# A recurrence with 64-step chunks, then a routed expert layer: other order of loads, zeroed pads, weights and last units

## The chip, the cores and the metric

The kernel runs on one core of a Trainium2 chip. The metric is the device time of one execution in microseconds (us), lower is better. The kernel before takes 865.59 us, the median of three runs (860.16 to 867.03).

The engines are TensorE (PE, with its weight loads shown apart as PEld), VectorE (DVE), ScalarE (ACT), GpSimd (POOL) and SyncE (SP), which here only issues DMAs. Each engine works through its own list of instructions in order. An instruction whose input is not ready holds up all that stands behind it on the same engine.

## The reference, cut to what matters

```python
for t in range(S):                                    # B=4, H=8, S=768, D=40
    y[:, :, t] = np.einsum('bhd,bhde->bhe', rt, state)
    Sa = np.einsum('bhde,bhe->bhd', state, at)
    state = state * wt[:, :, None, :] - np.einsum('bhd,bhe->bhde', Sa, bt) + np.einsum('bhd,bhe->bhde', vt, kt)
x = y.transpose(0, 2, 1, 3).reshape(3072, 320)
logits = x @ w_gate                                   # 8 experts
e = argmax(logits); g = softmax(logits)[e]
out = g * (relu(x @ w1[e]) @ w2[e])                   # w1: 8 x 320 x 1024, w2: 8 x 1024 x 320
```

A recurrence runs over 768 steps for 32 heads. Its output is the input of a layer in which each of 3072 rows goes to one of eight experts.

## The kernel before, in words

The work has three stages. The first is the recurrence, cut into chunks of 64 steps. A unit is one chunk of two batches with all their heads; there are 24 units (`NU`, line 316), and units 2c and 2c+1 are chunk c of the two pairs of batches. `unit(u)` (line 416) writes down the steps of one unit:

- seven loads, each of four DMAs of 40 KB (`load`, line 432): the decays `dec`, the vectors B and K into the one tile `KB`, A, V twice (`V2`, `Vu`) and R. For the first two units B, A and R are issued by ACT, all others by SP.
- preparation: a backward scan of the decays (`rv`, line 453), two small operations (line 457), a forward scan (`q`, line 461), both scans on DVE; two multiplications of halves of `KB` by `rv` (line 468) and one of A by `q` (line 470), on POOL.
- on TensorE the products of K and A and of B and A (lines 492 and 506), then a chain of squarings that inverts a triangular matrix (lines 518 to 584), the terms that need the state of the chunk before (lines 614 to 656), `p_z` (line 668), the output and new state `p_y` (line 692), and `p_x` (line 722), which turns the output into rows and multiplies it by the gate's weights. DVE and ACT copy or mask what comes out. SP stores the rows (line 758).

The heads of a tile are eight segments. In `dec`, A, `q`, `rv` and `pc` segment 2p+q holds pair p of batch q, so the segments of the two batches alternate. `dec` has segments of 65 columns, one for a reset and 64 decays. A DMA of `dec` fills the segments of one batch and one half of the partitions, so the two DMAs of a half interleave (`by_q`, line 440).

Tiles have pads (partitions 40 to 63 and 104 to 127) that must be zero, and in `dec` one. The tiles lie in rings of two or three buffers (lines 337 to 363), and lines 365 to 387 clear the pads of each buffer once. `fill_turn_gate` (line 158) prepares the gate's weights with two DMAs issued by POOL, `turn_sign` (line 166) negates them, and `route_constants` (line 137) makes the constants of the routing on POOL.

The order of this stage is made by a planner at build time, `in_order` (line 224). Each `Step` has a rank, an engine (or `ANY` for ACT or DVE), a guessed cost, and what it reads and writes (`Held`). The planner goes through time and takes the step that can start first; among those that can start at the same moment it takes the one of the lowest rank. The rank is the unit's number for the work of the unit, u-3 for its loads, u-1 for its preparation, u+1 for what follows `p_x`. For TensorE steps a term `uneven` is added to the rank: it compares a step's cost with its number of instructions `n` times `PACE`, so that steps with many short instructions alternate with steps of few long ones. What the planner guesses decides only the order. On the chip each instruction waits for its real inputs, which the framework finds from the regions that instructions write and read.

The weights of expert 0 are loaded by `fetch` (line 176) in four DMAs after half of the units (lines 767 to 772).

The second stage is the routing (lines 780 to 886), the third the experts (lines 889 to 987). There the weights of expert e+2 are loaded while e and e+1 run.

Of the kernel before, what the change touches and what calls it, by code (L numbers as in the profile page):

```python
# [23 lines left out]
def kernel(  # L24
# [151 lines left out]
    def fetch(pool, w1, w2):  # L176
# [4 lines left out]
        nc.sync.dma_start(t1[:], w1[: Dm - 64].rearrange("(a p) f -> p a f", p=128))  # L181
        for i in range(2):
            nc.sync.dma_start(
                t3[i * 64 : (i + 1) * 64], w1[Dm - 64 :].rearrange("p (k i f) -> i p k f", i=2, f=128)[i],
            )
        nc.sync.dma_start(t2[:], w2.rearrange("(a p) d -> p a d", p=128))
# [8 lines left out]
    PACE = 0.0134  # L195
# [28 lines left out]
    def in_order():  # L224
# [31 lines left out]
        while ready:  # L256
            times = sorted({f for f in bank_free if f is not None})
            best = None
            for s, r in ready.items():
                new = [h for h in s.ps if h.at is None]  # L260
                for e in ((ACT, DVE) if s.eng == ANY else (s.eng,)):
# [14 lines left out]
                    uneven = 2 * abs(even + s.cost - s.n * PACE) if s.n else 0.0  # L276
# [41 lines left out]
    with tc.tile_pool(name="ring", bufs=1) as ring, \  # L318
# [21 lines left out]
        r_KB = Ring("KB", [NP, 2, 2, C], 3, 2)  # L340
# [29 lines left out]
        for i, (t, held) in enumerate(r_dec.bufs):  # L370
# [45 lines left out]
        def unit(u):  # L416
# [9 lines left out]
            def head(t, p, q, par):  # L426
                return t[halves[par], 2 * p + q, :]
# [21 lines left out]
            load(other, 1 + A, by_q(Aq), hA)  # L449
# [14 lines left out]
            for i in range(2):  # L464
# [576 lines left out]
```

## Time and profile before

| What | Value |
|---|---|
| Runs of the kernel | 865.59 us median (860.16 to 867.03) |
| The profiled execution's own time | 866.43 us |
| Its span in the profile | 864.7 us |
| Granted TensorE clock, mean over the span | 0.946 |

The profile shows one execution. Times in it count from the start of its span; 1.7 us of the execution's own time lie outside the span. A granted clock of 1.00 is 2.4 GHz, 0.50 is 1.2 GHz; numbers between are means over a stretch in which both occurred. Busy time counts the time in which at least one instruction of the engine ran. A count of matmuls beside it (x) says how much was done. In a list of waits, "DVE rv L453 <- DMA dec" is idle time of DVE before an instruction of line 453, ended by the landing of a DMA into `dec`. A name such as SPq or ACTq is the sequencer of that engine, which issues DMAs.

### The profile page before, as it was taken

The page shows a single profiled execution, that of the slowest core. Times are in us where ns is not written, and L with a number is a line of the kernel's source. Part 1 is how long each engine was busy: PE and PEld are TensorE (multiplying, and loading weights), DVE is VectorE, ACT ScalarE, POOL GpSimd, SP SyncE. Part 2 cuts the span into 40 slices and gives each one's busy share as a digit, 9 for nine tenths or more (in the row PEclk, how much of TensorE's full clock was granted, in tenths as well). Part 3 has the DMA queues.
Part 4 walks back from the last instruction along what each step waited for, and adds up shares of the span by engine and source line. Part 5 has one row for each costly group of instructions (what it writes and reads, how often), then busy time and mean ns, then how long its engine had stood idle before and what let it go on. Part 6 is the DMA issues. An engine that isn't in the chain of part 4 may idle for free.

```text
span 864.7 us, 38029 instructions
## 1 busy us (share of the span) xinstructions
PE 767.2 (89%) x17128; PEld 607.9 (70%) x17128; DVE 464.2 (54%) x991; ACT 229.7 (27%) x495; POOL 178.5 (21%) x226
## 2 busy tenths in 40 slices
PE   0779899999999997999999997159999999999995
PEld 0668788989888997898889886147655655655643
DVE  8575688878888788687787773621120120120110
ACT  0233443434343442344333431001011111111010
POOL 9712101112012221121121100160401401101001
PEclk9998999999999999899999996566999999999999
DMA  3333323323232336323322100740424424202000
GB/s 86 81 68 68 69 51 70 84 51 88 59 76 62 78 76 172 72 63 73 82 62 64 29 13 11 226 146 10 148 68 136 140 68 147 77 6 87 16 7 24
DMA packets 136293, 65.16 MB, mean 75 GB/s; under 512 B 116585, under 2 KB 131967, under 8 KB 136128
## 3 DMA queue, kind: packets, MB, share of 16 engines
q1 hardware_dynamic: 128848, 52.26, 23.8%
q0 software_dynamic: 3200, 9.45, 3.5%
q8 instruction: 135, 2.21, 1.1%
q10 hardware_dynamic: 4080, 0.98, 0.5%
q14 instruction: 30, 0.25, 0.1%
HBM read 54.01 MB, written 9.31 MB: 73 GB/s over the span
## 4 chain that ended last, share of the span: by engine, by line
issue 36%; PE 32%; DVE 11%; POOL 8%; DMA 8%; SPq 3%; ACT 1%; POOLq 0%; DVEq 0%; ACTq 0%
PE ps L406 27%; DMA dec<-in_packed_dram 6%; POOL out_dram L936 3%; SPq L437 3%; PE ps L603 3%; POOL xg L894 3%; DVE X L516 2%; PE ps L593 2%; DVE X L513 1%; DVE q L461 1%; DVE rv L453 1%; DVE TT L516 1%; DVE M L573 1%; DVE ZU L676 1%; ACT X L401 1%
## 5 line engine op out<-in xcount | busy, mean ns | idle before, releaser
L406 PE MATMUL ps<-X 64*64 64x64 f32 (+1 forms) x6144 | 153.5, 243 | 10.2 <-issue 3.8
L406 PEld LDWEIGHTS ps<-X 64*64 64x64 f32 x6144 | 131.1, 136 | 22.5 <-issue 8.4
L920 DVE TENSOR_SCALAR h_sb<-hp 128x448 f32<-128x448 f32 (+2 forms) x44 | 21.8, 498 | 228.4 <-PE hp L919 221.7
L401 ACT COPY X<-ps 128x512 f32<-128x512 f32 x166 | 95.7, 587 | 157.0 <-PE ps L406 136.3
L929 PE MATMUL zp<-w,h_sb 128*128 128x320 f32 (+1 forms) x512 | 123.8, 433 | 0.0
L913 PE MATMUL hp<-xgT,w 128*128 128x448 f32 (+2 forms) x352 | 115.6, 476 | 4.0 <-DVE h_sb L920 3.9
L929 PEld LDWEIGHTS zp<-w,h_sb 128*128 128x128 f32 (+1 forms) x512 | 80.6, 177 | 37.4 <-issue 2.4
L913 PEld LDWEIGHTS hp<-xgT,w 128*128 128x128 f32 x352 | 61.6, 210 | 53.5 <-issue 48.0
L468 POOL TENSOR_TENSOR KB<-KB,rv 128x512 f32<-128x512 f32 x48 | 59.6, 1263 | 135.2 <-DMA KB<-in_packed_dram 65.2
L936 POOL DMA_INDIRECT out_dram<-zo,s_idx x28 | 27.7, 990 | 184.9 <-ACT zo L935 183.7
L470 POOL TENSOR_TENSOR A<-A,q 128x512 f32<-128x512 f32 x24 | 28.5, 1187 | 180.7 <-DVE g L742 59.3
L516 DVE TENSOR_TENSOR X<-ps,X 64x256 f32<-64x256 f32 x144 | 60.8, 422 | 3.2
L921 ACT ACTIVATE h_sb<-hp 128x448 f32<-128x448 f32 (+2 forms) x44 | 19.4, 442 | 161.3 <-PE hp L919 123.9
L406 PE MATMUL ps<-A,KB 64*64 64x64 f32 x1536 | 57.7, 229 | 4.3 <-DVE X L516 2.7
L406 PEld LDWEIGHTS ps<-A,KB 64*64 64x64 f32 x1536 | 53.1, 137 | 7.3 <-DVE X L516 3.1
L406 PE MATMUL ps<-R,Vu 64*128 64x64 f32 x768 | 51.6, 287 | 0.9 <-ACT Vu L661 0.7
L406 PEld LDWEIGHTS ps<-R,Vu 64*128 64x128 f32 x768 | 48.1, 199 | 3.9 <-ACT Vu L661 0.9
L513 DVE TENSOR_TENSOR X<-ps,X 128x256 f32<-128x256 f32 x72 | 30.1, 419 | 35.9 <-ACT X L401 35.6
L453 DVE TENSOR_TENSOR_SCAN rv<-dec,ones 128x521 f32<-128x521 f32 x24 | 30.5, 1270 | 32.0 <-DMA dec<-in_packed_dram 26.9
L935 ACT COPY zo<-zp 128x320 f32<-128x320 f32 x28 | 11.9, 426 | 119.8 <-PE zp L929 112.0
L406 PE MATMUL ps<-ZU,nKB 128*64 128x104 f32 (+1 forms) x768 | 39.9, 257 | 0.2
L894 POOL DMA_INDIRECT xg<-x_rows,g_idx x28 | 26.8, 958 | 54.3 <-PE tp L902 44.5
(182 smaller groups left out, 1096.0 us busy)
## 6 DMA issues: line engine op xcount, KB each, us to landing
w<-in_moe_w_dram SPq DMA_DIRECT2D x8, 1280.0 KB
w<-in_moe_w_dram SPq DMA_DIRECT2D x8, 1024.0 KB
KB<-in_packed_dram SPq DMA_DIRECT2D x184, 40.0 KB
x_rows<-xs SPq DMA_DIRECT2D x48, 96.0 KB
dec<-in_packed_dram SPq DMA_DIRECT2D x96, 40.0 KB
V<-in_packed_dram SPq DMA_DIRECT2D x96, 40.0 KB
Vu<-in_packed_dram SPq DMA_DIRECT2D x96, 40.0 KB
A<-in_packed_dram SPq DMA_DIRECT2D x88, 40.0 KB
```

Source lines behind the costliest of these rows:

```text
L401: nc.scalar.copy(dst, src)
L406: nc.tensor.matmul(out_, lhsT=lhsT, rhs=rhs, start=start, stop=stop, skip_group_check=True)
L437: (nc.sync if e == SP else nc.scalar).dma_start(dst(q, par), src)
L453: Step(pre, DVE, 1.4, lambda e: nc.vector.tensor_tensor_scan(rv[:, : SEG * C1 + 1][:, ::-1], dec[:, ::-1], ones65[:, ::-1], 0.0, op0=ALU.m ...
L468: Step(pre, POOL, 1.25, lambda e, kb=kb, by=by: nc.gpsimd.tensor_tensor(kb, kb, by, op=ALU.mult), reads=hrv, writes=hKB[i : i + 1])
L470: Step(pre, POOL, 1.22, lambda e: nc.gpsimd.tensor_tensor(Aq[:], Aq[:], q3[:, :, :C], op=ALU.mult), reads=hq, writes=hA)
L513: nc.vector.tensor_tensor(dst[:, 0], src[:, 0], old[:, 0], op=ALU.add)
L516: nc.vector.tensor_tensor(dst[o_, 1], src[o_ if o else halves[h], 1], old[halves[h], 1], op=ALU.add)
L894: nc.gpsimd.indirect_dma_start(out=xg[:, j, :], out_offset=None, in_=x_d[:, :], in_offset=bass.IndirectOffsetOnAxis(ap=gi, axis=0),)
L913: nc.tensor.matmul(hp[:, : c1 - c0], lhsT=w[0][:, db, (fb + i) * 128 : (fb + i + 1) * 128], rhs=xT[:, db, c0:c1], start=(db == 0), stop=False,
L929: nc.tensor.matmul(zp[r0 : r0 + n], lhsT=h[:, fb, c0 : c0 + n], rhs=w[2][:, fb, :], start=(fb == 0), stop=(fb == FB - 1), skip_group_check ...
L936: ins_ = nc.gpsimd.indirect_dma_start(out=out[:, :], out_offset=bass.IndirectOffsetOnAxis(ap=si, axis=0), in_=zo[:], in_offset=None, bound ...
```

## The change

- The segments of `dec`, A, `q`, `rv` and `pc` are numbered q*4+p in place of 2p+q, so that the segments of one batch lie side by side. The two multiplications of `KB` go by batch, not by pairs.
- In the planner `KB` has four parts; the loads of B and of K no longer order each other there.
- The pads of the buffers with index 1 and 2 are cleared at ranks near the units that first use them, no longer at ranks far below all units.
- The gate's weights are loaded by ACT, not by POOL, and negated by ACT. The constants of the routing are made after unit 20.
- `fetch` issues eight DMAs in place of four: two for the first 256 rows of w1, two for its last 64, four for w2. For expert 0 they are eight steps after units 4, 6, ... 18.
- The steps of the last unit have rank 22.1 in place of 23 (`rk`), so that units 22 and 23 have nearly the same rank.
- `PACE` is 0.013 (0.0134 before), and `uneven` is weighed by 3 (2 before).

```diff
     def fill_turn_gate(e):
         nc.gpsimd.memset(turn_gate[:, :, 128:], 0.0)
+        nc.gpsimd.tensor_copy(turn_gate[:, :, :128], ident[:, None, :].to_broadcast([128, NP, 128]))
+
+    def load_turn_gate(e):
         for par in range(2):
-            nc.gpsimd.dma_start(
+            nc.scalar.dma_start(
...
-        nc.gpsimd.tensor_copy(turn_gate[:, :, :128], ident[:, None, :].to_broadcast([128, NP, 128]))
     def turn_sign(e):
-        nc.gpsimd.tensor_scalar(turn_gate[:, :, 128:], turn_gate[:, :, 128:], scalar1=-1.0, scalar2=None, op0=ALU.mult)
+        nc.scalar.mul(turn_gate[:, :, 128:], turn_gate[:, :, 128:], -1.0)
...
-    def fetch(pool, w1, w2):
+    def fetch(pool, w1, w2, take=lambda part: part()):
...
-        nc.sync.dma_start(t1[:], w1[: Dm - 64].rearrange("(a p) f -> p a f", p=128))
+        for a in range(DB - 1):
+            take(lambda a=a: nc.sync.dma_start(t1[:, a], w1[a * 128 : (a + 1) * 128]))
...
-        nc.sync.dma_start(t2[:], w2.rearrange("(a p) d -> p a d", p=128))
+        for a in range(0, FB, 2):
+            take(lambda a=a: nc.sync.dma_start(t2[:, a : a + 2], w2[a * 128 : (a + 2) * 128].rearrange("(a p) d -> p a d", p=128)))
...
-    PACE = 0.0134
+    PACE = 0.013
...
-                    uneven = 2 * abs(even + s.cost - s.n * PACE) if s.n else 0.0
+                    uneven = 3 * abs(even + s.cost - s.n * PACE) if s.n else 0.0
...
-        r_KB = Ring("KB", [NP, 2, 2, C], 3, 2)
+        r_KB = Ring("KB", [NP, 2, 2, C], 3, 4)
...
-            Step(-100 + 9 * i, DVE, 1.2, fn, writes=held)
+            Step(i - 1.5 if i else -100, DVE, 1.2, fn, writes=held)
...
-                        zero(-99 + 9 * i + j, POOL if lo == 32 else DVE, 0.5 if r in (r_A, r_V2, r_R) else 0.9, t[lo : lo + 32], held)
+                        zero(i - 0.9 + j / 100 if i else j - 99, POOL if lo == 32 else DVE, 0.5 if r in (r_A, r_V2, r_R) else 0.9, t[lo : lo + 32], held)
         for i, (t, held) in enumerate(r_qini.bufs):
-            zero(-98 + 9 * i, POOL, 0.6, t[:], held)
+            zero(i - 0.9 if i else -98, POOL, 0.6, t[:], held)
         for r in (r_rhs, r_ST, r_S):
             for i, (t, held) in enumerate(r.bufs):
-                zero(-84 + 9 * i, POOL, 0.6, t[:], held)
+                zero(i + 0.1, POOL, 0.6, t[:], held)
         h_tg = Held()
-        Step(-80, POOL, 1.5, fill_turn_gate, writes=[h_tg], lag=3)
-        Step(-1, POOL, 0.2, turn_sign, writes=[h_tg])
-        Step(12, POOL, 8, route_constants)
+        Step(0.1, POOL, 0.8, fill_turn_gate, writes=[h_tg])
+        Step(-2, ACT, 0.8, load_turn_gate, writes=[h_tg], lag=4)
+        Step(0, ACT, 0.3, turn_sign, writes=[h_tg])
...
             def head(t, p, q, par):
-                return t[halves[par], 2 * p + q, :]
+                return t[halves[par], q * NP + p, :]
...
             def by_q(t):
-                return lambda q, par: t.rearrange("x (p q) j -> x q p j", q=2)[rows(par), q]
+                return lambda q, par: t[rows(par), q * NP : (q + 1) * NP]
             pre = u - 1
+            rk = min(u, NU - 1.9)
...
-            load(other, 1 + B_, lambda q, par: KB[rows(par), :, q, 1 - par, :], hKB)
-            load(SP, 1 + K, lambda q, par: KB[rows(par), :, q, par, :], hKB)
+            load(other, 1 + B_, lambda q, par: KB[rows(par), :, q, 1 - par, :], hKB[3:])
+            load(SP, 1 + K, lambda q, par: KB[rows(par), :, q, par, :], hKB[2:3])
...
-            for i in range(2):
-                ps_ = slice(2 * i, 2 * i + 2)
-                kb = KB[:, ps_].rearrange("x p q s j -> x (p q) s j")
-                by = behind[:, 4 * i : 4 * i + 4].unsqueeze(2).to_broadcast([128, 4, 2, C])
+            for q in range(2):
+                kb = KB[:, :, q]
+                by = behind[:, q * NP : (q + 1) * NP].unsqueeze(2).to_broadcast([128, NP, 2, C])
...
-            Step(u, PE, 1.0, p_ka, reads=hKB + hA, writes=[ps], n=64)
+            Step(rk, PE, 1.0, p_ka, reads=hKB + hA, writes=[ps], n=64)
...
         for u in range(NU):
             unit(u)
-            if u == NU // 2:
-                half_way = steps[-1]
-        def first_weights(e):
-            weights[0] = fetch(w_first, moe_w1[0], moe_w2[0])
-        Step(8, SP, 2.0, first_weights, after=[half_way])
+            ends.append(steps[-1])
+        Step(20, POOL, 8, route_constants, after=[ends[20]])
+        parts = []
+        weights[0] = fetch(w_first, moe_w1[0], moe_w2[0], parts.append)
+        for i, part in enumerate(parts):
+            Step(4 + 2 * i, SP, 0.4, lambda e, part=part: part(), after=[ends[4 + 2 * i]])
```

All steps of `unit` from `p_ka` to the output take `rk` for their rank in the same way.

## Rows read from the trace of the kernel before

**Rows 1.** The page: the span and the busy time of each engine

```profile
span 864.7 us, 38029 instructions
PE 767.2 (89%) x17128; PEld 607.9 (70%) x17128; DVE 464.2 (54%) x991; ACT 229.7 (27%) x495; POOL 178.5 (21%) x226
```

**Rows 2.** Windows: stretch, length, busy time and count of each engine, clock, DMA share, GB/s

```profile
24.00:120.00 96.00, 81.81 (x2591) 73.96 (x2593) 64.98 (x130) 33.65 (x68) 26.13 (x46) 0.91 0.30 69
120.00:330.00 210.00, 204.46 (x7053) 187.29 (x7045) 175.09 (x373) 86.53 (x187) 41.52 (x42) 1.00 0.31 70
330.00:355.00 25.00, 19.89 (x611) 17.43 (x604) 15.87 (x34) 9.39 (x20) 3.64 (x4) 0.86 0.58 155
355.00:510.00 155.00, 150.91 (x5161) 138.13 (x5157) 123.65 (x266) 58.86 (x127) 24.54 (x26) 1.00 0.26 59
510.00:547.00 37.00, 24.64 (x608) 21.80 (x600) 13.55 (x34) 8.14 (x21) 0.71 (x3) 0.72 0.08 18
547.00:865.00 318.00, 283.94 (x1152) 167.99 (x1152) 51.96 (x122) 31.29 (x72) 59.61 (x60) 0.92 0.28 88
```

**Rows 3.** Waits of DVE from 0 to 120 us, the longest: total, times, longest

```profile
DVE rv L453 <- DMA dec<-in_packed_dram: 21.8, 6, 5.9
```

**Rows 4.** Waits of SP's queue over the span, its waits for the decays

```profile
SPq L437 <- DMA dec<-in_packed_dram: 78.4, 48, 2.9
```

**Rows 5.** Timeline of the queues of SP and ACT, first loads: start, length, what

```profile
2.58 9.42 SPq L437 DMA_DIRECT2D dec<-in_packed_dram  x8
25.32 4.15 SPq L437 DMA_DIRECT2D dec<-in_packed_dram  x4
29.56 1.54 SPq L437 DMA_DIRECT2D KB<-in_packed_dram  x4
...
4.62 1.91 ACTq L437 DMA_DIRECT2D KB<-in_packed_dram  x4
```

**Rows 6.** Timeline of POOL, 0 to 62 us: start, length, what

```profile
3.65 0.94 POOL L367 MEMSET KB<- 32x1024 f32 x1
...
7.54 0.94 POOL L367 MEMSET KB<- 32x1024 f32 x1
...
21.00 3.33 POOL L468 TENSOR_TENSOR KB<-KB,rv 128x512 f32<-128x512 f32 x2
...
25.43 2.33 POOL L468 TENSOR_TENSOR KB<-KB,rv 128x512 f32<-128x512 f32 x2
...
28.83 0.20 POOL L139 MEMSET before<- 128x128 f32 x1
...
34.78 0.53 POOL L153 TENSOR_SCALAR tokv<-tokc 128x12 f32<-128x12 f32 x1
...
44.79 1.19 POOL L470 TENSOR_TENSOR A<-A,q 128x512 f32<-128x512 f32 x1 [4.59 <-DVE q L461]
```

**Rows 7.** Timeline of TensorE, 20 to 62 us: the first product of B and A

```profile
26.48 0.46 PE L406 MATMUL ps<-KB,A 64*64 64x64 f32 x8
```

**Rows 8.** Timeline of DVE, 0 to 62 us: the first two scans

```profile
13.30 1.24 DVE L453 TENSOR_TENSOR_SCAN rv<-dec,ones 128x521 f32<-128x521 f32 x1
...
17.22 1.24 DVE L461 TENSOR_TENSOR_SCAN q<-dec,qini 128x520 f32<-128x520 f32 x1
```

**Rows 9.** DMA queue of instructions, 305 to 330 and 330 to 355 us: packets, MB, share

```profile
q8 instruction: 7, 0.11, 1.9%
...
q8 instruction: 5, 0.08, 1.3%
```

**Rows 10.** Timeline, 500 to 547 us: TensorE's `p_z` of units 22 and 23, DVE

```profile
511.89 2.00 PE L406 MATMUL ps<-R,Vu 64*128 64x64 f32 x32
530.72 3.75 PE L406 MATMUL ps<-R,Vu 64*128 64x64 f32 x32 [0.72 <-ACT Vu L661]
...
526.29 0.69 DVE L573 TENSOR_TENSOR M<-ps,ihalf 128x512 f32<-128x512 f32 x1
534.50 1.29 DVE L676 TENSOR_TENSOR ZU<-ps,m_plus 128x512 f32<-128x512 f32 x2 [7.52 <-PE ps L406]
```

More of the change, by code (lines that the diff above doesn't have):

```diff
@@ L481, in masked @@
                 if by == DVE:
-                    Step(u, DVE, 0.69, lambda e: nc.vector.tensor_tensor(t, src(), mask, op=ALU.mult), reads=[ps], writes=held)
+                    Step(rk, DVE, 0.69, lambda e: nc.vector.tensor_tensor(t, src(), mask, op=ALU.mult), reads=[ps], writes=held)
                 else:
-                    Step(u, ACT, 0.59, lambda e: nc.scalar.copy(t, src()), reads=[ps], writes=held)
-                    Step(u, POOL, 1.2, lambda e: nc.gpsimd.tensor_tensor(t, t, mask, op=ALU.mult), writes=held)
+                    Step(rk, ACT, 0.59, lambda e: nc.scalar.copy(t, src()), reads=[ps], writes=held)
+                    Step(rk, POOL, 1.2, lambda e: nc.gpsimd.tensor_tensor(t, t, mask, op=ALU.mult), writes=held)
             def p_ka(e, ps=ps):
@@ L526, in p_sq @@
                             mm(pair(ps, C, w)[halves[s], q, p, :], l[halves[h], q, p, :], r[halves[h], q, p, :])
-            Step(u, PE, 8 * ROUND, p_sq, reads=hN1 + hT1, writes=[ps], n=128)
+            Step(rk, PE, 8 * ROUND, p_sq, reads=hN1 + hT1, writes=[ps], n=128)
             for i in range(2):
-                Step(u, ANY, 0.59, lambda e, i=i, ps=ps, X=X: copy(e, X[:, :, :, i, :], pair(ps, C, i)), reads=[ps], writes=hX[i : i + 1])
-            Step(u, DVE, 1.39, lambda e, X=X: sums(e, X[:, :, :, 2, :], ihalf[:, None, None, :].to_broadcast([128, 2, NP, C]), T1[:], False),
+                Step(rk, ANY, 0.59, lambda e, i=i, ps=ps, X=X: copy(e, X[:, :, :, i, :], pair(ps, C, i)), reads=[ps], writes=hX[i : i + 1])
+            Step(rk, DVE, 1.39, lambda e, X=X: sums(e, X[:, :, :, 2, :], ihalf[:, None, None, :].to_broadcast([128, 2, NP, C]), T1[:], False),
                  reads=hT1, writes=hX[2:3])
@@ L570, in p_end @@
                 p_power(e, pair(ps, C, 0), X, 1, 0)
-            Step(u, PE, 8 * ROUND, p_end, reads=hX, writes=[ps], n=128)
-            Step(u, DVE, 1.29, lambda e, ps=ps, X=X, TT=TT: sums(e, TT[:], pair(ps, C, 1), X[:, :, :, 2, :], True), reads=[ps] + hX[2:3], writes=hTT)
-            Step(u, DVE, 0.69, lambda e, ps=ps, M=M: nc.vector.tensor_tensor(M[:], pair(ps, C, 0), eye(2, NP), op=ALU.add), reads=[ps], writes=hM)
+            Step(rk, PE, 8 * ROUND, p_end, reads=hX, writes=[ps], n=128)
+            Step(rk, DVE, 1.29, lambda e, ps=ps, X=X, TT=TT: sums(e, TT[:], pair(ps, C, 1), X[:, :, :, 2, :], True), reads=[ps] + hX[2:3], writes=hTT)
+            Step(rk, DVE, 0.69, lambda e, ps=ps, M=M: nc.vector.tensor_tensor(M[:], pair(ps, C, 0), eye(2, NP), op=ALU.add), reads=[ps], writes=hM)
             TF, hTF = r_TF.take()
@@ L618, in unit @@
                 STq = ST[:, :, :, :D].rearrange("x p q d -> x q p d")
-                Step(u, DVE, 0.5, lambda e: nc.vector.tensor_tensor(
-                    STq, sa[:], pc[:].rearrange("x (p q) -> x q p", q=2).unsqueeze(3).to_broadcast([128, 2, NP, D]), op=ALU.mult,
+                Step(rk, DVE, 0.5, lambda e: nc.vector.tensor_tensor(
+                    STq, sa[:], pc[:].rearrange("x (q p) -> x q p", q=2).unsqueeze(3).to_broadcast([128, 2, NP, D]), op=ALU.mult,
                 ), reads=hsa + hpc, writes=hST)
@@ L673, in p_z @@
                                Vu[halves[q], p, 2 * par : 2 * par + 2, :].rearrange("x s t -> x (s t)"), R_[halves[q], p, par, :])
-            Step(u, PE, 1.93, p_z, reads=hV + huT + hR, writes=[ps], n=64)
+            Step(rk, PE, 1.93, p_z, reads=hV + huT + hR, writes=[ps], n=64)
             for s in range(2):
-                Step(u, DVE, 0.69, lambda e, s=s, ps=ps: nc.vector.tensor_tensor(
+                Step(rk, DVE, 0.69, lambda e, s=s, ps=ps: nc.vector.tensor_tensor(
                     ZU[:, s, :, :C], psum[:, ps.at + s, :].rearrange("x (b j) -> x b j", j=C),
@@ L701, in p_y @@
                                start=(c == 0 and p == 0))
-            Step(u, PE, (0.5 if c else 0) + 16 * 0.95 * w / 1000, p_y, reads=hnKB + (hZU[:2] if last else hZU) + (hSn + hR if c else []), writes=[psy], n=128 if c else 64)
+            Step(rk, PE, (0.5 if c else 0) + 16 * 0.95 * w / 1000, p_y, reads=hnKB + (hZU[:2] if last else hZU) + (hSn + hR if c else []), writes=[psy], n=128 if c else 64)
             if not last:
```

63 lines of the change are left out of this document (32 added, 31 removed).

## The prediction

> **What bounds the kernel now.** I read the page first. TensorE is busy for 89% of the span [rows 1], so the question is where it is not, and how much it does when it is. The windows by stage answer both, because they count matmuls beside busy time [rows 2]. From 120 to 330 us TensorE starts 7053 matmuls in 210 us, 33.6 per us at full clock, and from 355 to 510 us 5161 in 155 us, 33.3. That is the pace of the undisturbed stage. Four stretches fall short of it, and I price each by that pace, 33.6:
>
> - Before 24 us TensorE has nothing to do. The first product of B and A starts at 26.48 us [rows 7].
> - From 24 to 120 us it starts 2591 matmuls, worth 77.1 us. Of 96 us, 18.9 are lost.
> - From 330 to 355 us it starts 611, worth 18.2 us. Of 25 us, 6.8 are lost.
> - From 510 to 547 us it starts 608, worth 18.1 us. Of 37 us, 18.9 are lost, part of them because the clock is at 0.72 in the mean.
>
> Routing and experts take the last 318 us [rows 2], and in them TensorE's work stays as it was. So the change can win from some 24 + 18.9 + 6.8 + 18.9 = 69 us, and only a part of each.
>
> The waits tell what stands in the first two stretches. DVE stood 21.8 us in six waits before the backward scan, each ended by a DMA into the decays [rows 3]. While DVE stands there, the masks and sums of the units ahead stand behind the scan, and TensorE waits for those. SP's queue shows why the decays are late: it waited 78.4 us in 48 waits for a DMA of the decays, two waits in each of the 24 loads [rows 4]. An undisturbed load of four DMAs takes 1.54 us to issue, that of the decays 4.15 us [rows 5]. The third stretch begins as the first expert's weights are loaded. The fourth is the last unit alone.
>
> **The change part by part.** Times are those of the profiled execution: 864.7 us of span, 866.4 us in all.
>
> *Start.* POOL clears pads and prepares the gate from 3.65 to 21.00 us before it multiplies for the first time. The pads of index 0 alone end where those of index 1 begin, at 7.54 us [rows 6]. With only these in front, the first unit goes as follows. SP issues the decays from 2.58 us in 1.54 us, to 4.1. The two waits of an old load make 4.15 - 1.54 = 2.6 us, 1.3 each, beyond an issue of some 0.4, so a DMA lands about 1.7 us after its issue begins: at 5.8 us. The scan takes 1.24 us, the forward scan as much [rows 8], with small operations about 9 us. B is issued by ACT up to 6.5 us [rows 5] and K by SP after the decays up to 6.2, so `KB` has landed at 8.3. POOL multiplies it in 3.33 us where scans run beside it (2.33 where they don't) and A in 1.19 [rows 6], to 12.8 us. I take 15 us for the first product in place of 26.48, since POOL and DVE must also clear the next buffers in the gaps and ACT must wait for the pads of A: **-11 us**. Nothing slipping would give -13.5. If all 3.9 us of pads of index 1 stand before the multiplications and their loads slip in turn, -6. The clears of index 1 and 2 are the same instructions as before, moved to where DVE and POOL wait. The two DMAs and the sign of the gate move to ACT: two issues of 0.4 us and an operation, before the loads of unit 1 there; POOL loses the same. They are needed only by the first `p_x`, at no cost either way within 1 us.
>
> *Ramp.* A unit's 28 issues keep SP busy for seven times 1.6 us, and the decays cost 2.6 us more, which now go. For the first three units SP has four, four and then, for the third, its decays, B, K and A: 12 loads of 1.6 us from 2.6 us, 21.8 us, landed by 23.5, multiplied by 27. Before, the multiplication of A for the third unit began at 44.79 us [rows 6], 18.3 us after the first product; now it comes about 12 after it. Units thus enter six us closer together, and DVE no longer stands before scans for decays that the planner expected earlier. What is late next is K and B of the third unit, and the clears before them. Of 18.9 us lost, the 21.8 us of DVE's waits cover all, but a start with one and two units cannot fill TensorE. I take **-8 us**; bounds 0 (loads of other tiles end the same waits) and -14.
>
> *First weights.* In equal windows of 25 us, the queue that brings instructions moved seven packets from 305 to 330 us and five from 330 to 355 [rows 9], 16 KB each. The ratio of matmuls is alike, 611 to 840 (25 times 33.6). So TensorE ran at the rate at which its instructions came, while DMA was busy at 0.58 in the mean. Eight DMAs over units 4 to 18 move the same bytes, so the collision is spread, not gone. One that falls between two packets of instructions costs nothing. Half of the loss, rounded down, gives **-3 us**; bounds -6.8 (all hidden) and +6 (each of eight pieces costs 1.6 us). The issue itself, 0.4 us in every other unit, lies in a queue with 28 issues of loads, 11 us, in a unit of 19.9 us (16,024 matmuls of rows 2 for 24 units at 33.6 per us).
>
> The Trainium skill, in "Runtime: NRT & Kernel Launch", section "Instruction fetch mechanics", says that the sequencer fetches the next block of 256 instructions by its own DMA queue while it executes, and that crossing a block is mostly hidden. The packets of 16 KB agree with the block; the seven and five packets beside 840 and 611 matmuls do not agree with "hidden" where weights move. If the rule held, cutting the weights would give nothing, and the sum would come out at 841.
>
> *Last units.* Unit 23 leaves its chain of squarings with `M` at 526.29 us and the stage ends at 547 [rows 2, 10], 20.7 us. Before that, units 22 and 23 were both there, but 22 always came first. `p_z` shows the price of the clock: 2.00 us for unit 22, 3.75 for unit 23 [rows 10]: TensorE is busy 24.64 of these 37 us [rows 2], and the clock fell to 1.2 GHz. DVE waited 7.52 us for it. With nearly equal ranks the squarings of both run side by side, and then each one's `p_z`, `p_y`, `p_x` fill the other's gaps. The last chain stays, because each of its steps needs the one before. I keep two thirds of the 18.9 us: **-6.5 us**; bounds 0 (same tail, later unit 22) and -12.
>
> *Evenness.* `PACE` and the weight of `uneven` reorder TensorE's steps everywhere. Nothing in the trace shows the new order. TensorE idles 5.5 us of 210 and 4.1 of 155 [rows 2], so a better order could give some -6 us; I take 0 and +6 as the other end.
>
> *The rest at 0.* The routing's constants take 6.5 us of POOL, from 28.83 to 35.31 [rows 6], now after unit 20; the last multiplications of A could stand behind them (+3). The experts' weights come in eight DMAs, not four, some 2 us more issue per expert, behind 1152 matmuls in 318 us; a gap would cost 2. The multiplications by batch have the same shape and count.
>
> **Sum.** -11 - 8 - 3 - 6.5 = -28.5, so 866.4 - 28.5 = 837.9 us by the profiled execution. The median of the runs is 0.8 us below that execution, which gives **837 us**.
>
> **The rivals.**
>
> *Only the start pays.* Pieces of weights cost what the block cost (0, not -3) and the tail is bounded by its chain at the low clock (0, not -6.5): 847. For it: the bytes are the same, and `p_z` at 3.75 us shows how the tail pays for a low clock.
>
> *Start and ramp both near their ends:* -13, -14, -5 and -11 make 823. For it: all of DVE's long waits in the ramp name one cause. Against it: one unit cannot fill TensorE.
>
> *The instructions came late for another reason than the weights:* then the pieces give nothing, the other terms stay, and 866.4 - 25.5 make 841. Against it: five packets for seven just there. The section of the Trainium skill quoted above would have it so.
>
> *The false order goes, and the queue is still the bound.* SP's issues alone, 1.6 us a load, hold the third unit: -6, 0, -3, -6.5 and +2 for late loads make 853. Against it: 44.79 us is far behind what 12 loads need.
>
> *Slower.* With weight 3, a mismatch of one third of the planner's microsecond outweighs a whole unit's rank. Then TensorE takes steps of younger units ahead of the older one's, the chain from `p_rhs` to `p_y` stretches, and the rings hold the loads back. The place is 120 to 510 us, 12,825 matmuls; it decides from a pace of 30.9 per us on, where 12,825 take 415 us in place of 385 and eat the whole gain. At 30.3 the time is 876. Against it: TensorE idles only 3% there, and weight 2 could already outweigh a rank.
>
> **How the numbers follow.** Forecast 0.60 (827 to 848 by its own terms), only the start 0.15, both ends 0.10, another reason 0.08, queue 0.04, slower 0.03. The range 822 to 855 takes in all but the slower case and the outer parts of the others. This kernel's measurement tells about 1% from no change, 8.6 us. All cases but the slower one lie under 857; I leave 0.05 of their 0.97 for terms that all fall to their short ends together. That makes faster 0.92, within 1% 0.05, slower 0.03.
>
> **What would show it.** Right: no waits of SP for the decays; the first product of B and A at 13 to 17 us; DVE's waits before the scan gone from the first 120 us; some 3200 matmuls by 120 us in place of 2602; no 20 us stretch at half pace; the routing beginning near 519 us in place of 547, with `p_z` of both last units near 2 us. Wrong: waits for `KB` in place of those for `dec` in the ramp; a pace under 33 between 120 and 510 us; a last stretch still 20 us long after `M`; or a slow stretch behind each piece of the weights.

## The result and the profile after

The changed kernel takes 833.41 us, the median of four runs (829.77 to 834.8). The kernel before, run beside it, takes 866.31 us (860.16 to 867.27). The ratio is 0.9628, with a 95% interval of 0.9573 to 0.9683: faster by 3.7%. The forecast was 837 us.

The profiled execution took 829.77 us, the fastest of the four. It is compared with the one of before, 866.43 us. The page, its span and busy times, beside [rows 1]:

```profile
span 827.7 us, 38051 instructions
PE 748.2 (90%) x17128; PEld 589.7 (71%) x17128; DVE 461.9 (56%) x977; ACT 235.9 (28%) x510; POOL 175.4 (21%) x223
```

TensorE issues the same 17128 matmuls in a span that is 37 us shorter. The busy share hardly moves (89% to 90%). That is why the windows by stage have to be read, and in them the counts. They stand in the columns of [rows 2]:

```profile
0.00:24.00 24.00, 9.45 (x213) 8.39 (x214) 17.27 (x37) 3.36 (x6) 22.66 (x46) 1.00 0.46 100
24.00:120.00 96.00, 86.86 (x3034) 78.48 (x3031) 82.62 (x168) 38.25 (x80) 23.39 (x21) 1.00 0.36 81
120.00:484.00 364.00, 344.74 (x11832) 312.74 (x11824) 289.93 (x601) 151.10 (x324) 64.67 (x67) 1.00 0.31 72
484.00:521.00 37.00, 29.88 (x920) 27.56 (x920) 20.00 (x51) 11.81 (x30) 5.23 (x30) 0.97 0.10 25
521.00:828.00 307.00, 277.24 (x1152) 162.53 (x1152) 52.04 (x122) 31.34 (x72) 59.46 (x60) 0.94 0.29 91
```

By 120 us TensorE has started 213 + 3034 = 3247 matmuls, where 7 + 2591 = 2598 stood in before. Between 24 and 120 us it does 443 more in the same 96 us. In the last 37 us of the stage it does 920 in place of 608, at a clock of 0.97 in place of 0.72. The recurrence's stage ends 26 us earlier. The last stage is 11 us shorter. Of the change only the eight DMAs of an expert's weights reach it. I come back to that.

TensorE's timeline, the first product of B and A, stood at 26.48 us in [rows 7]:

```profile
17.02 0.46 PE L410 MATMUL ps<-KB,A 64*64 64x64 f32 x8
```

POOL's timeline shows what is still in front of it, beside [rows 6]:

```profile
6.63 0.94 POOL L371 MEMSET Vu<- 32x1024 f32 x1
7.52 0.94 POOL L371 MEMSET KB<- 32x1024 f32 x1
...
10.57 0.61 POOL L160 COPY turn_gate<-ident 128x512 f32<-128x512 f32 x1
11.15 3.25 POOL L473 TENSOR_TENSOR KB<-KB,rv 128x512 f32<-128x512 f32 x2
14.46 0.52 POOL L371 MEMSET A<- 32x512 f32 x1
...
15.52 1.18 POOL L475 TENSOR_TENSOR A<-A,q 128x512 f32<-128x512 f32 x1
```

From 7.52 us on, clears of the next buffers and the copy of the gate fill 3.6 us ahead of the first multiplication. Two more clears stand between it and that of A. Before, the first multiplication began at 21.00 us.

SP's queue waited 78.4 us for the decays in [rows 4]. Now that group has 2 waits and 0.6 us. Near the top of its waits now stand those of a load for TensorE, which must first have read the buffer that the load fills (36.4 us in 61 waits before):

```profile
SPq L441 <- PE ps L410: 83.0, 72, 8.2
```

DVE's waits for the decays from 0 to 120 us, 21.8 us in [rows 3]:

```profile
DVE rv L459 <- DMA dec<-in_packed_dram: 1.2, 1, 1.2
```

The tail, TensorE's `p_z` beside [rows 10], then DVE:

```profile
492.20 2.00 PE L410 MATMUL ps<-R,Vu 64*128 64x64 f32 x32 [0.78 <-ACT X L405]
506.00 3.79 PE L410 MATMUL ps<-R,Vu 64*128 64x64 f32 x64
```

```profile
502.42 0.69 DVE L578 TENSOR_TENSOR M<-ps,ihalf 128x512 f32<-128x512 f32 x1
...
508.03 1.29 DVE L681 TENSOR_TENSOR ZU<-ps,m_plus 128x512 f32<-128x512 f32 x2
509.82 1.29 DVE L681 TENSOR_TENSOR ZU<-ps,m_plus 128x512 f32<-128x512 f32 x2 [0.50 <-PE ps L410]
...
521.06 0.36 DVE L791 TENSOR_TENSOR sc<-lgn,lmin 128x192 f32<-128x192 f32 x1 [3.98 <-DMA x_rows<-xs]
```

Both last units issue their `p_z` in one go, 64 matmuls in 3.79 us. Half of that is the 1.9 us of the full clock; the last one alone took 3.75 us before. The wait of 7.52 us before `ZU` is 0.50 us. From the last `M` to the routing's first operation it is 18.6 us, 20.7 before.

### The profile page after: what moved, and what is told of

It reads as the page before. It is cut to its first block, busy times and chain, and to the rows that moved or that the text cites. A ratio compares the mean times of both kernels' runs of the same rounds, so it can differ in the third digit from the quotient of the medians.

```text
span 827.7 us, 38051 instructions
## 1 busy us (share of the span) xinstructions
PE 748.2 (90%) x17128; PEld 589.7 (71%) x17128; DVE 461.9 (56%) x977; ACT 235.9 (28%) x510; POOL 175.4 (21%) x223
## 4 chain that ended last, share of the span: by engine, by line
PE 47%; issue 33%; DVE 7%; POOL 7%; DMA 3%; ACT 1%; SPq 1%; POOLq 0%; DVEq 0%; ACTq 0%
PE ps L410 40%; PE ps L608 4%; POOL out_dram L944 3%; POOL xg L902 3%; PE ps L598 2%; DVE X L521 1%; DVE q L467 1%; ACT X L405 1%; DMA xg<-x_rows,g_idx 1%; DMA x_rows<-xs 1%; SPq L441 0%; DVE X L518 0%; DVE TT L521 0%; DVE oh_c L867 0%; DVE pc L465 0%
## 5 line engine op out<-in xcount | busy, mean ns | idle before, releaser
L921 PE MATMUL hp<-xgT,w 128*128 128x448 f32 (+2 forms) x352 | 110.5, 457 | 0.0
L921 PEld LDWEIGHTS hp<-xgT,w 128*128 128x128 f32 x352 | 57.0, 193 | 48.7 <-issue 46.4
L929 ACT ACTIVATE h_sb<-hp 128x448 f32<-128x448 f32 (+2 forms) x44 | 19.4, 442 | 152.2 <-PE hp L927 152.2
L475 POOL TENSOR_TENSOR A<-A,q 128x512 f32<-128x512 f32 x24 | 30.4, 1266 | 148.0 <-DVE q L467 123.4
L410 PE MATMUL ps<-R,Vu 64*128 64x64 f32 x768 | 47.8, 275 | 0.9 <-ACT X L405 0.8
L410 PEld LDWEIGHTS ps<-R,Vu 64*128 64x128 f32 x768 | 44.7, 188 | 2.8 <-ACT X L405 0.9
L943 ACT COPY zo<-zp 128x320 f32<-128x320 f32 x28 | 11.9, 425 | 118.6 <-PE zp L937 118.6
L410 PEld LDWEIGHTS ps<-ZU,nKB 128*64 128x64 f32 x768 | 34.5, 137 | 4.9 <-issue 3.3
L927 PE MATMUL hp<-xgT,w1c 64*128 64x448 f32 (+2 forms) x176 | 36.4, 490 | 0.0
```

The source lines that it names most:

```text
L410: nc.tensor.matmul(out_, lhsT=lhsT, rhs=rhs, start=start, stop=stop, skip_group_check=True)
L475: Step(pre, POOL, 1.22, lambda e: nc.gpsimd.tensor_tensor(Aq[:], Aq[:], q3[:, :, :C], op=ALU.mult), reads=hq, writes=hA)
L921: nc.tensor.matmul(hp[:, : c1 - c0], lhsT=w[0][:, db, (fb + i) * 128 : (fb + i + 1) * 128], rhs=xT[:, db, c0:c1], start=(db == 0), stop=False,
L927: nc.tensor.matmul(hps[i][:, : c1 - c0], lhsT=w[1][hf, fb // 2, :], rhs=xT[hf, DB - 1, c0:c1], start=False, stop=True)
```

## The experiments

**How they are compared.** One measure serves all profiles: a stretch's length less its matmuls at 33.6 per us, the pace of [rows 2]. This is the time that TensorE lost there. The stretches are 0 to 24 us, 24 to 120 us, 120 us to 37 us before the routing's first operation, and the last 37 us before it. "Route" is when that operation starts, "rest" what follows of the span. The runs were made on several chips, on which the kernel before has medians from 856.0 to 867.4 us. So times are compared by their ratio to the kernel before on the same chip, or by medians of one chip: u_seg, u_zero, u_block, u_pace, after_again, a_seg_zero, u_rank_pace and start2 ran on one, a_seg, u_rank and before_again on another. On the second the ratio of the medians is higher than the ratio given (0.977 for a_seg, 0.971 for u_rank); both lie in the intervals. A profile is one execution, and the same kernel's routing start moved by 3 us from one profile to the next. That of a_seg, 844.68 us, is the slowest of its four runs (the others take 833.3 to 837.58).

| Kernel | First product | Lost in the four stretches | Route | Rest | Ratio (95%) |
|---|---|---|---|---|---|
| before | 26.48 | 23.8, 18.9, 9.0, 18.9 | 547.0 | 317.7 | 1 |
| before_again | 26.31 | 23.8, 19.8, 12.4, 18.1 | 550.0 | 306.8 | 0.9999 (0.996 to 1.0039) |
| after | 17.02 | 17.7, 5.7, 11.8, 9.6 | 521.1 | 306.6 | 0.9628 (0.9573 to 0.9683) |
| after_again | 17.02 | 17.7, 6.2, 8.5, 9.6 | 518.4 | 315.0 | 0.9671 (0.9626 to 0.9717) |
| a_seg | 26.32 | 23.7, 7.0, 7.7, 18.3 | 532.8 | 310.1 | 0.9727 (0.9658 to 0.9796) |
| a_seg_zero | 21.32 | 20.9, 0.5, 11.3, 19.6 | 529.1 | 314.7 | 0.9803 (0.9769 to 0.9837) |
| u_seg | 17.45 | 19.8, 17.5, 15.4, 9.6 | 538.5 | 316.5 | 0.9901 (0.9868 to 0.9934) |
| u_zero | 24.92 | 23.6, 4.3, 12.0, 11.6 | 527.6 | 317.6 | 0.9825 (0.9758 to 0.9893) |
| u_block | 17.04 | 17.9, 9.3, 7.9, 9.6 | 521.1 | 314.1 | 0.9682 (0.9616 to 0.9748) |
| u_pace | 17.02 | 17.9, 4.8, 6.7, 17.4 | 523.1 | 314.7 | 0.9739 (0.9675 to 0.9803) |
| u_rank | 17.02 | 17.2, 5.9, 11.9, 12.4 | 523.7 | 307.8 | 0.9679 (0.9614 to 0.9744) |
| u_rank_pace | 17.02 | 17.7, 4.4, 4.6, 18.2 | 521.0 | 314.5 | 0.9733 (0.9702 to 0.9763) |
| start2 | 15.66 | 15.8, 8.9, 5.3, 14.6 | 520.6 | 317.6 | 0.9737 (0.9701 to 0.9773) |
| mix | 17.05 | 17.6, 5.4, 9.7, 12.1 | 521.1 | 316.3 | 0.968 (0.9633 to 0.9726) |

**The order between the decays' DMAs: undone (u_seg) and alone (a_seg).** u_seg is the changed kernel with the old numbering of segments. The planner's order stays:

```diff
-                return t[halves[par], q * NP + p, :]
+                return t[halves[par], 2 * p + q, :]
...
-                return lambda q, par: t[rows(par), q * NP : (q + 1) * NP]
+                return lambda q, par: t.rearrange("x (p q) j -> x q p j", q=2)[rows(par), q]
```

The views of `rv`, `pc` and `q` follow in the same way. a_seg puts the new numbering alone into the kernel before, with that kernel's order of work; the two multiplications of `KB` go by batch in it.

> The changed kernel with the segments in their old order (2p+q); the planner's order of all steps is untouched, so only the layout differs. Theory (the false order is what held the decays back): SP waits for the decays again, 48 times, DVE waits before the scan again, the first product comes 2 to 3 us later and the ramp loses another 6 to 8 us: 842 to 845 us. Rival (the pads held the start, the layout is secondary): 833 to 836 us.

> The kernel before with the new order of the segments alone; the planner's order of all steps is that of before. Theory (false order held the ramp): DVE's waits before the scan in the first 120 us fall from 21.8 to under 5 us, and the time falls by 7 to 11 us: 855 to 859 us. Rival (without the other ranks of the clears the loads stay late): 863 to 867 us.

The waits of u_seg's SP queue, and its windows before 120 us; then the same stretch of a_seg:

```profile
SPq L441 <- DMA dec<-in_packed_dram: 78.2, 50, 2.8
```

```profile
0.00:24.00 24.00, 6.84 (x140) 6.41 (x144) 16.60 (x34) 2.10 (x3) 19.20 (x41) 0.99 0.36 79
24.00:120.00 96.00, 81.45 (x2637) 72.96 (x2631) 72.59 (x145) 36.03 (x74) 25.42 (x25) 0.91 0.34 76
```

```profile
24.00:120.00 96.00, 90.44 (x2991) 82.52 (x2993) 75.40 (x151) 38.92 (x81) 28.44 (x48) 0.95 0.32 72
```

With the old numbering the 78 us of waits are back in SP's queue. The first product stays at 17.45 us, and yet the ramp loses 17.5 us, nearly the 18.9 of before. With the new numbering alone the first product stays at 26.32 us, and the ramp loses 7.0. So the numbering sets most of what the ramp loses, with the old start and with the new one. The routing starts 17 to 20 us later with it undone, and 14 to 17 us earlier with it alone. By the ratio, undoing it takes back most of the gain (0.9901); alone it gives 2.7% (2.3% between the medians). Both expectations had the direction right and the size too small: 854.47 us for 842 to 845, and 836.11 us for 855 to 859. In u_seg the waits reach beyond 120 us as well: DVE's waits for the decays from 120 to 480 us sum to 16.0 us in five, where before has 5.2 in three up to 510 us. The longest, 4.3 us, lies in the stretch from 245 to 270 us, which has 591 matmuls, where others have some 800:

```profile
245.00:270.00 25.00, 21.39 (x591) 19.07 (x588) 14.19 (x32) 7.76 (x17) 6.08 (x6) 0.93 0.30 69
```

Two things narrow the cause. The queue of the loads moves the same 128848 packets in before and in a_seg, so the loads are cut as before and only their order is freer. And alternating is not enough: the segments of A alternate in before as well, but SP's queue shows no wait of A for A, and a load of A issues in 1.54 us. What `dec` alone has are segments of 65 columns of which a load fills 64. That the framework orders the two DMAs because of this is likely and not tested.

**The clears: undone (u_zero), and added to a_seg (a_seg_zero).**

```diff
-            Step(i - 1.5 if i else -100, DVE, 1.2, fn, writes=held)
+            Step(-100 + 9 * i, DVE, 1.2, fn, writes=held)
...
-                zero(i + 0.1, POOL, 0.6, t[:], held)
+                zero(-84 + 9 * i, POOL, 0.6, t[:], held)
```

The two other calls of `zero` change alike. a_seg_zero goes the other way: a_seg with the new ranks.

> The changed kernel with the ranks of the clears as before (all far below the units). Theory (the pads held the start): the first product of B and A comes at about 24 us in place of 17.0, and the end moves by the same 6 to 8 us: 840 to 842 us. Rival (the loads hold the start and the pads hide behind them): first product at 17 to 19 us, 833 to 835 us.

> The kernel before with the new order of the segments and the new ranks of the clears, nothing else. Theory (these two are nearly the whole gain; the clears add 4 to 7 us to the layout alone): first product near 17 us, the routing at 525 to 529 us, ratio 0.963 to 0.969. Rival (pieces, ranks and evenness carry the rest): routing at 530 us or later, ratio 0.971 or more.

u_zero's first product starts at 24.92 us, as expected, and the time is 1.5 to 2% above that of the changed kernel (0.9825 to 0.9671 and 0.9628), more than expected: on one chip 847.83 us to 835.08, or 12.8 us. The first product is 7.9 us later. The stretch before 24 us loses 5.9 us more, and the ramp makes up 1.4. The other two stretches are a little worse; of the 12.8 us, some 4.5 lie in start and ramp, and where the rest comes from is not shown. In a_seg_zero the first product comes only at 21.32 us, since on POOL the gate still stands in front:

```profile
8.09 1.59 POOL L161 DMA_DIRECT2D turn_gate<-in_moe_w_gate_dram  x2 [0.32 <-POOL turn_gate L159]
9.73 0.61 POOL L164 COPY turn_gate<-ident 128x512 f32<-128x512 f32 x1
...
15.97 0.94 POOL L367 MEMSET KB<- 32x1024 f32 x1
17.00 2.31 POOL L467 TENSOR_TENSOR KB<-KB,rv 128x512 f32<-128x512 f32 x2
```

Its ramp then loses 0.5 us only, and start and ramp gain 9.3 us on a_seg. The middle and the tail give back 4.9 of that. By the timed runs it is not faster than a_seg (0.9803 and 0.9727, on two chips). The theory for it (a ratio of 0.963 to 0.969) failed. Why the clears pay 1.5% or more in the changed kernel and nothing here is not settled. What a_seg_zero lacks against u_rank_pace, on the same chip, is the gate on ACT, the four parts of `KB`, the later constants and the weights in pieces. Together they move the first product from 21.32 to 17.02 us, the routing from 529.1 to 521.0 and the median from 845.63 to 839.6. Apart from the pieces none of them was undone alone.

**The first weights (u_block).** The eight pieces in one step, after unit 12:

```diff
-        for i, part in enumerate(parts):
-            Step(4 + 2 * i, SP, 0.4, lambda e, part=part: part(), after=[ends[4 + 2 * i]])
+        def all_parts(e):
+            for part in parts:
+                part()
+        Step(8, SP, 3.2, all_parts, after=[ends[12]])
```

> The changed kernel with the eight DMAs of the first expert's weights issued together after unit 12. Theory (the same bytes take the same time from the instructions' queue, spread or not): 832 to 835 us, with one stretch of 25 us that loses 6 to 7 us and less loss elsewhere. Rival (pieces fit between the packets of instructions and save 3 us or more): 836 to 840 us.

The routing starts at 521.08 us (521.06), and the ratio is 0.9682. The windows of u_block, the stretch in which the weights move and the one behind it:

```profile
320.00:345.00 25.00, 21.01 (x747) 19.19 (x740) 18.22 (x41) 10.57 (x25) 1.66 (x3) 1.00 0.55 150
345.00:370.00 25.00, 24.42 (x858) 22.57 (x856) 20.87 (x44) 9.52 (x21) 3.76 (x4) 1.00 0.34 78
```

The block costs 25 - 747 / 33.6 = 2.8 us in its stretch and nothing in the next. Laid two us later, from 322 to 347 us, the stretch has 696 matmuls and loses 4.3. So the pieces can win some 3 to 4 us at most. By time nothing is seen of it: the medians are 835.73 us and 835.08 (after_again), on one chip, between the two outcomes expected, and the intervals reach 0.5 to 0.7% to either side. In the changed kernel no stretch of 25 us from 120 to 470 us has fewer than 774 matmuls, but twelve of the fourteen have fewer than the 840 of the undisturbed pace. That the pieces cause this is not shown: they are issued at 163, 198, 250, 284, 327, 361, 412 and 446 us, and the stretch with the fewest, 220 to 245 us, has none.

**The last units (u_rank, u_pace, u_rank_pace).** u_rank has `rk = u`. u_pace has the old pace and weight, u_rank_pace has both:

```diff
-    PACE = 0.013
+    PACE = 0.0134
...
-                    uneven = 3 * abs(even + s.cost - s.n * PACE) if s.n else 0.0
+                    uneven = 2 * abs(even + s.cost - s.n * PACE) if s.n else 0.0
```

> The changed kernel with the last unit at its old rank (23). Theory (the last unit alone leaves TensorE idle and at 1.2 GHz): the stretch from the last M of the squarings to the routing is 18 to 21 us long again, the time 840 to 843 us. Rival (the tail was shortened by the order that the rest of the change made): 832 to 835 us.

> The changed kernel with PACE 0.0134 and weight 2 as before. Theory (the new evenness costs the 3 us that the middle stretch lost): 829 to 831 us, 120 to 484 us at 33 matmuls per us or more. Rival (it makes no difference): 832 to 835 us. Second rival (it pays): 838 us or more.

> The changed kernel with both the old rank of the last unit and the old PACE and weight. Singly each left the routing only 2 to 3 us later. Theory (rank and evenness are two ways to the same short tail, and either one alone gives most of it): with both undone the last 37 us lose 18 us or more, and the routing begins at 527 us or later. Rival (they are independent and small): 525 to 526 us.

The last two stretches of u_rank_pace, in the windows:

```profile
120.00:483.95 363.95, 351.93 (x12073) 320.94 (x12076) 295.80 (x618) 149.98 (x322) 67.20 (x92) 1.00 0.31 72
483.95:520.95 37.00, 24.74 (x631) 21.97 (x620) 13.28 (x36) 7.36 (x19) 0.71 (x3) 0.70 0.08 18
```

Its tail is that of before (631 matmuls, clock 0.70). Its middle does 12073 matmuls in the length in which the changed kernel does 11832. With the new rank alone the tail is still old (u_pace, 17.4); with the new pace alone it is mostly new (u_rank, 12.4). TensorE's last `p_z` and DVE's wait for it show the same, first in u_pace, then in u_rank:

```profile
506.89 3.75 PE L410 MATMUL ps<-R,Vu 64*128 64x64 f32 x32 [0.72 <-DMA x_rows<-xs]
510.66 1.29 DVE L681 TENSOR_TENSOR ZU<-ps,m_plus 128x512 f32<-128x512 f32 x2 [6.78 <-PE ps L410]
```

```profile
510.20 2.00 PE L410 MATMUL ps<-R,Vu 64*128 64x64 f32 x32
512.23 1.29 DVE L681 TENSOR_TENSOR ZU<-ps,m_plus 128x512 f32<-128x512 f32 x2
```

So the shorter tail comes from the pace first, then the rank. In these profiles the middle gives it back, within the 3 us by which profiles differ: the routing starts at 520.95 us with both undone. Neither outcome expected of u_rank_pace came (527 us or later, 525 to 526), and u_rank did not get the long tail that was expected of it. The timed runs put the old pace and weight some 0.6% behind (0.9733 and 0.9739 to 0.9671 for the changed kernel again), with intervals that overlap or nearly touch.

**The changed kernel with a freer start (start2).** All clears that the first unit does not need at once (those of the buffers 1 and 2, of `rhs`, `ST` and `S`, and DVE's of R and `Vu`) and the gate wait for that unit's scan or its second multiplication of `KB`:

```diff
+            if u == 0:
+                for s in later:
+                    s.deps.add(steps[-1] if s.eng == POOL else scanned)
```

> The changed kernel with every clear that the first unit does not need held back until the first unit's backward scan (on DVE) or its multiplications of KB (on POOL). In the profile of the changed kernel POOL cleared for 2.6 us more when the data of KB could be multiplied, and DVE for 2 us more when the decays had landed. Theory (these clears are what the start still waits for): the first product at 13 to 15 us in place of 17.0, the routing 2 to 4 us earlier. Rival (the second unit's loads then come later and eat it): first product earlier, routing at the same time or later.

The first product comes at 15.66 us, 1.4 us earlier. But the second unit's multiplication of `KB` moves from 19.60 to 22.64 us: POOL's clears now end at 21.7 us there, and it then waits 0.96 us for DVE's scan. The ramp loses 8.9 us in place of 6.2, and the routing starts 2.2 us later than in the changed kernel's profile on that chip (after_again), with a ratio of 0.9737 to 0.9671, whose intervals overlap. So the rival's outcome came, by way of the clears and not of the loads that it named. The clears have to go somewhere.

**Old pace for most units, new for the last (mix).**

```diff
+    def pace_of(s):
+        return PACE if s.rank[0] >= LATE else PACE0
...
-                    uneven = 3 * abs(even + s.cost - s.n * PACE) if s.n else 0.0
+                    uneven = (3 if s.rank[0] >= LATE else 2) * abs(even + s.cost - s.n * pace_of(s)) if s.n else 0.0
```

`PACE0` is 0.0134, `LATE` is 19.

> The changed kernel with the old pace and weight (0.0134, 2) for the steps of the units with a rank below 19, and the new ones (0.013, 3) from rank 19 on, so that only the last units are planned for evenness. Theory: with the old pace the stretch from 120 us to 37 us before the routing lost 4.6 to 6.7 us where the new pace lost 11.8, and the new pace gives its gain in the last 37 us (9.6 lost, 17.4 to 18.2 without); so the two add up: about 5 to 7 lost in the middle, about 10 at the end, the routing starts at 514 to 518 us (521.1 in the changed kernel's profile), and the ratio to the kernel before is 0.962 or less. Rival: what the end gains is work that the middle has to give up, whatever the pace; then the losses of the two stretches together stay near 21 to 23 us, the routing starts at 519 to 523 us and the ratio is 0.967 to 0.974.

```profile
120.00:484.09 364.09, 347.51 (x11906) 315.59 (x11902) 289.76 (x604) 148.89 (x322) 66.23 (x87) 1.00 0.31 72
484.09:521.09 37.00, 29.05 (x838) 25.45 (x829) 19.43 (x49) 10.35 (x25) 2.28 (x11) 0.91 0.08 19
```

These are its two last windows: 9.7 and 12.1 us lost, 21.8 together. The rival held. The start of the routing is where it was, and the ratio of 0.968 is inside the intervals of the changed kernel. The two gains do not add up.

**Both kernels once more (before_again, after_again).**

> The kernel before, unchanged, for a second profile. From the routing's first operation to the end the profile of before took 317.7 us and that of after 306.6 us, though no step there got shorter. Theory (a chance stop of TensorE of 4 us in the first expert and the low clock after it, in that one execution): about 307 us here. Rival (the change removed something that stops TensorE there): 315 to 319 us here too.

> The changed kernel, unchanged, beside the next three on one chip. Theory (the stop of TensorE in the first expert comes and goes by chance and costs up to 11 us): the routing begins at 518 to 524 us as in the first profile, the rest takes 306 us without the stop or up to 317 with it, and the ratio to before is 0.960 to 0.970. Rival (the change prevents the stop): the rest takes 306 to 308 us in any profile of this kernel.

They were run to see what changes from one profile to the next of one kernel. The rest of the span does, by 8 to 11 us, as both theories had it. In before, DVE's and ACT's waits in the first expert, and TensorE's timeline there, the groups of eight matmuls of a row of the first layer:

```profile
DVE h_sb L920 <- remote: 5.4, 1, 5.4
...
ACT h_sb L921 <- remote: 4.8, 1, 4.8
```

```profile
578.11 1.16 PE L913 MATMUL hp<-xgT,w 128*128 128x128 f32 x8
...
585.57 2.08 PE L913 MATMUL hp<-xgT,w 128*128 128x128 f32 x8 [3.87 <-DVE h_sb L920]
...
588.30 2.07 PE L913 MATMUL hp<-xgT,w 128*128 128x128 f32 x8
```

In the changed kernel's profile there is no such wait, and the groups go on at full clock:

```profile
552.82 1.16 PE L921 MATMUL hp<-xgT,w 128*128 128x128 f32 x8
...
555.84 1.16 PE L921 MATMUL hp<-xgT,w 128*128 128x128 f32 x8
```

"Remote" means that the profile cannot name the releaser. TensorE stands for 3.87 us, and from 585.57 to 593.7 us its granted clock is 0.50, which is 1.2 GHz: a group takes 2.07 us in place of 1.16. The stop is also in after_again (6.3 and 4.3 us), u_seg, u_zero, u_block, u_pace, a_seg_zero, u_rank_pace, start2 and mix. It is not in before_again, after, u_rank and a_seg. With it the rest takes 314.1 to 317.7 us, without it 306.6 to 310.1. So it comes and goes with the same kernel, and the change neither made nor removed it. Whether it comes by chance is not shown: it is in all eight profiles of one chip and in none of the three of another. Like beside like: with the stop 866.43 (before) to 835.48 us (after_again), 31.0 less. Without it 858.56 (before_again) to 829.77 us (after), 28.8 less. These pairs are not known to come from one chip each; between medians of one chip the kernels differ by 32.9 us (the result) and 28.1 (863.19 to 835.08). What releases the two engines is open.

The second profile of before also puts the slow stretch of [rows 2] in question. There SP issues the four DMAs of the first weights from 336.90 us, in before from 332.63. The stretch laid as far ahead of them as in [rows 2]:

```profile
334.30:359.30 25.00, 21.50 (x714) 19.52 (x716) 17.17 (x38) 10.33 (x22) 3.66 (x4) 0.93 0.58 154
```

With the same DMA share it has 714 matmuls in place of 611.

## Why the prediction was right, point by point

The forecast was 28.5 us less by the profiled execution. Between the medians of one chip the kernel is 32.9 us faster at the result and 28.1 at after_again; between profiles of like kind it is 28.8 and 31.0. The time was right, and so were the places of the two largest terms, start and ramp. The third, the last units, was put down to the wrong part of the change. The sizes were off in ways that cancel: by the profile the start was too large, the ramp and the last stretch too small, the weights not borne out. That the sum came so near is partly luck. Nor do the parts add up as I had added them: undone one at a time on one chip, the numbering costs 19.4 us, the clears 12.8, the pace 5.0 and the pieces 0.7. That is 38 us without the rank, the gate and the rest, where the whole change is worth 28.1.

- *Start, -11.* The first product moved by 9.5 us, between my -11 and the -6 of all clears of index 1 in front. The place was right: POOL's clears and the gate. I had allowed 2.2 us for clears; 3.6 us stand in front of the first multiplication and 1.0 more before that of A. But I priced each microsecond of the first product as one of time. The stretch before 24 us won 6.1 us only, u_zero loses 4.5 in start and ramp for 7.9 of the first product, and start2 wins 1.4 there and nothing behind it. The runs say more than the start, though: u_zero takes 12.8 us longer than the changed kernel, most of it behind the ramp and not explained.
- *Ramp, -8.* The cause was right, the size too small: the stretch won 13.2 us (18.9 to 5.7), and a_seg alone, with the old start, wins 11.9. I had bounded it at -14, and took less because "a start with one and two units cannot fill TensorE"; that sentence belonged to the start. Together start and ramp won 19.3 us, where I had put 19. The waits for the decays after 120 us, 16.0 us of them in u_seg, are no part of it: before had 5.2 there, and its middle lost no more than that of the changed kernel.
- *First weights, -3.* Not borne out. The term took the loss of the slow stretch, 6.8 us, as one that pieces would halve. That loss was partly of the one execution: in before_again the same four DMAs leave 714 matmuls in their 25 us, a loss of 3.8. u_block has the weights in one block and is as fast; the block costs it 2.8 to 4.3 us in its stretch, and the changed kernel loses as much in the middle without it (11.8 and 8.5 us to 7.9). A gain below 3 us is inside the noise of these runs. In the changed kernel the packets of instructions in 320 to 345 us are six beside 794 matmuls, in u_block six beside 747. They follow the matmuls and do not tell which of them holds the other. The Trainium skill's "mostly hidden" ("Runtime: NRT & Kernel Launch", "Instruction fetch mechanics") is not decided by these runs; the outcome that I had derived from it for this term, that cutting gives nothing, came about as far as these runs can tell.
- *Last units, -6.5.* The last stretch won 9.3 us, as both `p_z` run at the full clock and DVE waits 0.50 us in place of 7.52. But I had named the nearly equal ranks for this, and put the pace at 0. With the new rank and the old pace the last `p_z` takes 3.75 us and DVE waits 6.78 (u_pace); with the old rank and the new pace it takes 2.00 and DVE does not wait (u_rank). The rank gives 0.8 of the 9 us without the new pace and 2.8 with it. And little of this is time saved: with both undone the routing starts at 520.95 us, where the changed kernel's profiles have 521.06 and 518.37, and the medians differ by 4.5 us (839.6 to 835.08), with intervals that overlap. That this term fits is luck.
- *Evenness, 0.* The middle lost 11.8 us in the changed kernel's profile and 8.5 in the next, 9.0 before. The 0 holds within what profiles differ. But it stands for two things that cancel: the old pace has a better middle (4.6 to 6.7) and a worse tail.
- *The rest at 0.* The routing's constants are made on POOL at 493 us, while it idles. The last stage's 11 us are the stop, no effect of the change.

Of the rivals, "only the start pays" was right about the pieces; its 0 for the tail is wrong for the last stretch, and nearer than my -6.5 to what rank and pace changed of the routing's start. "Both ends" named the ramp's true size. The slower one, weight 3, did not come: the middle goes at 11832 / 364 = 32.5 matmuls per us, above the 30.9 from which it would have decided.

Of the signs that I named, nearly all are there: SP's waits for the decays gone, the first product at 17.02 us (the edge of 13 to 17), 3247 matmuls by 120 us (some 3200; for before the windows give 2598, not 2602), the routing at 521 us (near 519), no stretch at half pace, and `p_z` at the full clock. Two lie on the wrong side or near it. The pace between 120 us and the last stretch is 32.5 matmuls per us, under the 33 that I had named; but it was 32.8 in before too (12800 in 390 us), so this sign could not tell. And the stretch after `M` is 18.6 us long, near 20.

## What to carry to other kernels

A DMA that fills alternating segments of a tile, with a column left out in each, can wait for the DMA that fills the others, although they share no element (`dec` here, while A alternated without a wait): look in the issuing queue's waits for a load that waits for its own kind, and lay the tile out by what one DMA writes. Price a stretch by its matmuls at the pace of the undisturbed stage, not by busy time, and check a term by undoing that part alone: here terms of the wrong size gave a right sum. When two parts aim at one stretch, undo each and both: here the pace did what the rank was meant to do. A gain in the last units that a planner's weight buys can be paid in the middle, so look at both before it is counted.

## What the runs showed of the hardware that was not expected

- A wait of 3.4 to 7.4 us in the first expert, released by something that the profile calls remote, is in ten of fourteen profiles and comes and goes with the same kernel. With the 1.2 GHz after it (2.07 us for a group of 1.16), the rest of the span takes 4 to 11 us more: up to a third of what this change is worth, so a single profile can mislead by that much.
- 4 DMAs of weights at once (a_seg) leave 700 matmuls in the 25 us in which they move, 8 DMAs at once (u_block) 747, with DMA busy at 0.56 and 0.55. In [rows 2] it was 611, in before_again 714. The pace thus falls with the block, by 2.8 to 6.8 us, and cutting it in eight over the stage wins nothing that these runs can tell.
